# A retention layer and two expert layers in one kernel: carry and inner product summed in PSUM, a table made on chip, low bits on ScalarE, PSUM divided, late loads held back

## The chip, the cores and the metric

The kernel runs on one core of one Trainium2 chip. The metric is the device time of one execution in microseconds; of the kernel before, three runs took 606.27, 607.22 and 610.22 us, the median being 607.22.

## The reference, cut to what matters

```python
# q, k, v: [2, 8, 768, 64] float32
gamma = 1.0 - 2.0 ** (-5.0 - np.arange(H))
for t in range(S):                       # retention, state per (batch, head): 64 x 64
    state = gamma[None, :, None, None] * state + einsum('bhd,bhe->bhde', k[:, :, t], v[:, :, t])
    y[:, :, t] = scale * einsum('bhd,bhde->bhe', q[:, :, t], state)
x = y as [1536 tokens, 512]
h = x @ w_in;  x = (max(h, 0) + log1p(exp(-abs(h)))) @ w_out         # layer 0, d_ff = 2048
h = x @ w_in2; x = (h * clip(h + 3, 0, 6) / 6) @ w_out2              # layer 1, d_ff = 2048
```

The four weight matrices arrive as float64. Every product is computed to nearly float32 exactness, from operands that are split into a high half of reduced precision (fp32r) and a low half, the rest.

## The kernel before, in words

**Retention.** The sequence is cut into chunks of 128 tokens, six per batch, so there are 12 units, counted from 0 (`attend`, line 368). A unit loads k, q and v (256 KB each, `load`, line 392). TensorE turns k and q by transposes (called T below, `turned`, line 408); ScalarE copies k out of PSUM (kT) and VectorE multiplies q by the table `tq_sb` (qT). VectorE scales v (vs). TensorE forms scores in two halves (S, `scores`, line 426), and VectorE masks them (pt). TensorE forms the state's increments (D, `product`, line 440), and VectorE adds them to the running states (st, lines 449 to 466). Then come the carry product from the states (C, `carry`, line 468, into a bank `oc`) and the inner product of pt and vs (I, `inner`, line 478, into two banks `oi`). ScalarE copies `oc` to a buffer of the pool e, VectorE adds the banks `oi` to it into a buffer of the pool g (lines 496 to 508), ScalarE rounds this to the high half `x_hi`, and VectorE subtracts for the low half `x_lo` (lines 509 to 511).

**Expert layers.** Tokens are taken in three blocks of 512, d_ff in 16 slices of 128. `gemm1` (line 517) is a block of 12 products of 512 columns into one bank h, `gemm2` (line 555) a block of 12 into four accumulator banks. Between them ScalarE and VectorE apply the activation and split it into `hi` and `lo`. There are 96 blocks of each of the two.

**Weights.** 64 weight slices (`weight`, line 229) are fetched as words of 64 bits (512 KB) into one of three buffers `raw`. ScalarE scales the high word and VectorE clamps it; the low word's bits are added either by ScalarE (`bits`, a Relu activation, line 257) followed by `sign` and `shift` on VectorE, or by VectorE alone (`shifted`, `sign`, `merge`). `BITS` (line 148) chooses: VectorE alone for every fourth slice. The result `cv` is split into the halves `w`: for the slices that `BY_DVE` (line 145) names VectorE subtracts (`low`), for the others ScalarE writes the negative and an accumulating DMA from POOL's queue adds (`add`).

**The order.** A planner (`Plan`, line 24) is given every task with its engine, cost, due time and the buffers and banks that it takes and gives back. `run` (line 70) issues, on the engine that can start first, the task with the earliest due time among those that can start about as soon. So the kernel's text does not show the order; all engine calls go through `keep_in_program_order` (line 41), which is why every row of the profile bears L41. The banks of PSUM are one pool of eight, which `places` (line 61) hands out: to a task of two banks two neighbours, else the banks that are free first. SP's queue carries all loads in order, POOL's the accumulating DMAs.

The lines that set due times of the units in TensorE's order are these:

```python
for i, block in enumerate(([("Tk", u), ("Tq", u)], [("D", u)], [("S", u)], [("C", u), ("I", u)])):
    gaps.setdefault(start + int((4 * n + i) * per), []).extend(block)
```

Of the kernel before, what the change touches and what calls it, by code (L numbers as in the profile page):

```python
# [22 lines left out]
class Plan:  # L23
# [5 lines left out]
    class Task:  # L29
        def __init__(self, n, eng, cost, fn, after, due, take, give, load):  # L30
# [13 lines left out]
    def __init__(self, tc):  # L44
        self.tc, self.tasks, self.pools, self.users, self.slot = tc, [], {}, {}, {}
        self.tensor, self.vector, self.scalar, self.gpsimd, self.sync = (
            self.Engine(self, getattr(tc.nc, e)) for e in ("tensor", "vector", "scalar", "gpsimd", "sync"))
# [6 lines left out]
    def add(self, eng, cost, fn, after=(), due=0.0, take=(), give=(), load=0.0):  # L54
        t = self.Task(len(self.tasks), eng, cost, fn, after, due, take, give, load)
        self.tasks.append(t)
        for k in t.give:
            self.users.setdefault(k, []).append(t)
        return t

    def places(self, pool, keys, at=None):

        times = [(x if at is None else max(x, at), i) for i, x in enumerate(self.pools[pool]) if x is not None]
        if len(keys) == 2:
            have = {i: x for x, i in times}
            two = min(((max(x, have[i + 1]), -i) for i, x in have.items() if i + 1 in have), default=None)
            return two and [-two[1], 1 - two[1]]
        return [i for _, i in sorted(times)[:len(keys)]] if len(times) >= len(keys) else None

    def run(self, log=None):  # L70
        free = {"PE": 0.0, "DVE": 0.0, "ACT": 0.0, "POOL": 0.0, "SP": 1.2}
        line = 0.0
        todo = {e: sorted((t for t in self.tasks if t.eng == e), key=lambda t: (t.due, t.n)) for e in free}
        left = {k: len(v) for k, v in self.users.items()}
        for _ in self.tasks:
            best = None
            for e, ts in todo.items():
                found = []
                for t in ts[:80]:
                    if any(a.done is None for a in t.after):  # L80
                        continue
                    at = max([free[e]] + [a.done + (self.LAG[a.eng] if a.eng != e else 0.0) for a in t.after])
# [22 lines left out]
            if t.load:  # L105
                line = max(line, end + 1.2) + t.load
                end = line + 0.5
# [17 lines left out]
def kernel(ctx, tc, q, k, v, w1_in, w1_out, w2_in, w2_out, tq, tk, tcc, out):  # L125
# [17 lines left out]
    AHEAD = 3  # L143

    def BY_DVE(n):
        return n < 6 or n < 2 * NF and n % 3 == 1

    def BITS(n):
        return n % 4 != 1
# [26 lines left out]
    nc.pool("bank", 8)  # L176
    conv = [[("conv", m, i) for i in range(9)] for m in range(2)]
# [21 lines left out]
    for u in range(START):  # L199
        pe += [("S", u), ("D", u)] + ([("Tk", u + 1), ("Tq", u + 1)] if u + 1 < START else []) + [("C", u), ("I", u)]  # L200
# [7 lines left out]
    spread(range(START, FIRST), 0, 1.0)  # L208
# [126 lines left out]
    small = fixed.tile([P, HALF + H + NP], F32, name="small")  # L335
    mask, tk_sb, tc_sb = small[:, :HALF], small[:, HALF:HALF + H], small[:, HALF + H:]
# [14 lines left out]
    def table(dst, src, when):  # L351
        return nc.add("SP", 0.45, lambda: nc.sync.dma_start(out=dst, in_=src), [], when, load=1.3 if dst is tq_sb else 0.1)

    def both(keys):
        a, b = sorted(nc.slot[x][1] for x in keys)
        return banks[:, a:b + 1:b - a, :NP * HALF].rearrange("p x (n t) -> p x n t", n=NP)

    def sub(keys, j):
        i = sorted(nc.slot[x][1] for x in keys)[j]
        return banks[:, i, :NP * HALF].rearrange("p (n t) -> p n t", n=NP)  # L360
# [4 lines left out]
    part = [slice(j * HALF, (j + 1) * HALF) for j in range(2)]  # L365
    tables, ready = {}, {}

    def attend(u):
# [6 lines left out]
        def task(eng, cost, fn, after, when, take=(), give=(), load=0.0):  # L375
            return nc.add(eng, cost, fn, after, when, [(p, k) for p, k in take], list(give) + mine, load)
# [15 lines left out]
        def load(n, when, parts=1):  # L392
            return task("SP", 0.45 * parts, fetch(n, parts), [], when, take=own(n), load=1.32)
# [9 lines left out]
        if u == 0:  # L403
            tables["q"] = table(tq_sb, tq, begin + 2)
            tables["k"] = table(tk_sb, tk, begin + 2.1)
            tables["c"] = table(tc_sb, tcc, begin + 3.1)

        def turned(n):
# [5 lines left out]
        tp = task("PE", cost["Tk"], turned("k"), [ik], d["Tk"], take=[("bank", ("kP", u))])  # L414
# [3 lines left out]
        qt = task("DVE", PSX, lambda: nc.vector.tensor_tensor(tile_of("qT"), bank(("qP", u)), tq_sb, ALU.mult), [tp, tables["q"]],  # L418
# [3 lines left out]
            [iv, tables["k"]], d["D"] - 1.2, take=own("vs"), give=[("v", u)])  # L422

        sc, ds, oi = ([(n, j, u) for j in range(2)] for n in ("sc", "ds", "oi"))

        def scores():
# [7 lines left out]
            tile_of("pt").rearrange("p n (g t) -> p g n t", g=2).rearrange("p g n t -> p g n t"), both(sc),  # L434
            mask.rearrange("p (a n t) -> p a n t", a=1, n=1).to_broadcast([P, 2, NP, HALF]), ALU.mult), [s],
            d["I"] - 1.2, take=own("pt"), give=sc)
# [20 lines left out]
        if not last:  # L457
# [8 lines left out]
            ready["end", u] = task("DVE", 0.42, faded, [e, tables["c"]], due["C", u + 1] - 2.0, give=[end[1]])  # L466
# [8 lines left out]
        c = task("PE", cost["C"] / (1 + first), carry, [qt, sm, None if first else ready["end", u - 1]], d["C"],  # L475
                 take=[("bank", ("oc", u))], give=[mid[1], ("qT", u)] + ([] if first else [("end", u - 1)]))

        def inner():
            for h in range(H):
                g, p = h % 2, h // 2  # L480
                for j in range(2):
                    nc.tensor.matmul(sub(oi, j)[part[g], p, :], tile_of("vs")[part[j], h, :], tile_of("pt").rearrange(
                        "p n (g t) -> p g n t", g=2)[part[j], g, p, :])

        n = task("PE", cost["I"], inner, [pt, vs], d["I"], take=[("bank", x) for x in oi], give=[("pt", u), ("vs", u)])
# [4 lines left out]
        def split(t):  # L490
            return t.rearrange("p n (j t) -> p j n t", j=2)

        def of(n):
            return at_slot((n, u)).rearrange("p (n t) -> p n t", n=NP)

        if first:
            o0 = task("ACT", 0.35, lambda: nc.scalar.activation(split(of("on"))[:, 0], sub(oi, 0), AF.Copy), [n], d["I"] + 0.7,
                      take=[("g", ("on", u))], give=oi)
            o1 = task("ACT", 0.35, lambda: nc.scalar.activation(split(of("oe"))[:, 1], split(bank(("oc", u)))[:, 1], AF.Copy), [c],
                      d["I"], take=[("e", ("oe", u))], give=[("oc", u)])  # L500
# [155 lines left out]
```

## Time and profile before

| | us |
|---|---|
| median of three runs | 607.22 |
| the profiled execution, its own time | 606.65 |
| its span, first to last instruction | 604.5 |
| TensorE busy | 582.9 |
| VectorE busy | 335.9 |
| ScalarE busy | 304.7 |
| POOL busy | 44.3 |

The span is what the views of the trace cover; 2.15 us of the execution lie around it. Instructions of one engine overlap a little, so starts, not ends, tell how fast a queue moves. PE is TensorE, DVE VectorE, ACT ScalarE, SP the queue of loads and stores. A time in brackets is idle time of the engine before an instruction, with the instruction that ended it.

### The profile page before, as it was taken

Reading aid. Unit: us, or ns where it says so; the run is one execution under the profiler, and the core shown is the slowest. Engines: PE = TensorE matmul, PEld = TensorE weight load, DVE = VectorE, ACT = ScalarE, POOL = GpSimd, SP = SyncE. Lnnn points to the kernel's source line nnn. Section 1 sums busy time; section 2 is a strip of 40 time slices with the busy share of each in tenths; the row PEclk is TensorE's granted clock in tenths of the full one; section 3 lists DMA queues with packets and bytes.
Section 4 is the critical chain, followed back from the end, with each engine's and each line's share of the span. In section 5 each row is a group of like instructions: output and inputs, shape, how many; then the busy total and the mean of one; then the engine's idle time right before and its main releaser. Section 6 shows DMA issues by size and latency. Waiting matters only on the chain.

```text
span 604.5 us, 9654 instructions
## 1 busy us (share of the span) xinstructions
PE 582.9 (96%) x3891; PEld 478.2 (79%) x3891; DVE 335.9 (56%) x584; ACT 304.7 (50%) x516; POOL 44.3 (7%) x57
## 2 busy tenths in 40 slices
PE   7698889999999999999999999999999999999997
PEld 6576668878788888888888887888888888888886
DVE  4899898995655333376677985622422222322223
ACT  2468877994533333476779996622222222222220
POOL 0001111120000000011122221100000000000000
PEclk9899989999999999999999999999999999999999
DMA  8997776966210100046588987510100000100001
GB/s 193 237 252 199 195 183 158 241 180 137 54 37 21 51 0 1 1 105 157 152 196 212 247 211 176 130 18 0 71 1 1 0 1 0 71 0 1 0 1 69
DMA packets 68364, 59.87 MB, mean 99 GB/s; under 512 B 39776, under 2 KB 56416, under 8 KB 68320
## 3 DMA queue, kind: packets, MB, share of 16 engines
q1 hardware_dynamic: 61264, 46.41, 26.9%
q0 software_dynamic: 7056, 12.85, 12.4%
q8 instruction: 30, 0.49, 0.4%
q14 instruction: 14, 0.11, 0.1%
HBM read 43.26 MB, written 3.15 MB: 77 GB/s over the span
## 4 chain that ended last, share of the span: by engine, by line
PE 76%; DVE 10%; DMA 6%; ACT 5%; issue 3%; SPq 1%; DVEq 0%; ACTq 0%
PE banks L41 76%; DVE cv L41 5%; DMA raw<-in_moe_w_out_dram 3%; DMA raw<-in_moe_w_in_dram 2%; DVE raw L41 1%; ACT w L41 1%; DVE g L41 1%; DVE lo L41 1%; ACT raw L41 1%; DMA v<-in_v_dram 1%; ACT cv L41 1%; ACT e L41 1%; SPq L41 1%; DVE x_lo L41 1%; DVE w L41 1%
## 5 line engine op out<-in xcount | busy, mean ns | idle before, releaser
L41 PE MATMUL banks<-x_hi,w 128*128 128x512 f32 x768 | 254.8, 393 | 5.0 <-ACT kT L41 2.2
L41 PEld LDWEIGHTS banks<-x_hi,w 128*128 128x128 f32 x768 | 144.8, 189 | 37.1 <-DVE g L41 2.5
L41 PE MATMUL banks<-x_lo,w 128*128 128x512 f32 x384 | 150.2, 391 | 0.0
L41 PE MATMUL banks<-hi,w 128*128 128x512 f32 x384 | 127.5, 393 | 0.8 <-ACT w L41 0.5
L41 PE MATMUL banks<-w,hi 128*128 128x512 f32 (+1 forms) x386 | 118.3, 388 | 0.0
L41 DVE SCALAR_TENSOR_TENSOR g<-e,banks 128x512 f32<-128x512 f32 x48 | 33.0, 688 | 114.1 <-ACT e L41 114.0
L41 ACT ACTIVATE e<-banks,three 128x512 f32<-128x512 f32 x48 | 32.9, 686 | 124.6 <-PE banks L41 116.7
L41 DVE SCALAR_TENSOR_TENSOR cv<-raw,cv 128x512 uint32<-128x512 uint32 x128 | 87.5, 689 | 6.7 <-ACT cv L41 4.2
L41 DVE TENSOR_TENSOR lo<-g,hi 128x512 fp32r<-128x512 f32 x96 | 66.2, 690 | 44.7 <-ACT hi L41 43.4
L41 ACT ACTIVATE hi<-g 128x512 fp32r<-128x512 f32 x96 | 60.5, 630 | 49.8 <-DVE g L41 33.3
L41 PEld LDWEIGHTS banks<-hi,w 128*128 128x128 f32 x384 | 72.0, 188 | 17.0 <-ACT w L41 0.9
L41 PEld LDWEIGHTS banks<-x_lo,w 128*128 128x128 f32 x384 | 72.6, 189 | 14.7
L41 PEld LDWEIGHTS banks<-w,hi 128*128 128x128 f32 x386 | 72.4, 188 | 14.9
L41 ACT ACTIVATE w<-cv 128x512 fp32r<-128x512 f32 x113 | 68.3, 624 | 16.7 <-DVE cv L41 16.2
L41 PE MATMUL banks<-lo,w 128*128 128x512 f32 x192 | 75.1, 391 | 1.4 <-DVE lo L41 1.4
L41 PE MATMUL banks<-w,lo 128*128 128x512 f32 (+1 forms) x193 | 74.9, 388 | 0.0
L41 POOL DMA_DIRECT2D w<-cv x49 | 43.3, 887 | 348.9 <-ACT w L41 208.3
L41 ACT ACTIVATE g<-banks 128x512 f32<-128x512 f32 (+1 forms) x50 | 29.2, 584 | 54.7 <-PE banks L41 54.2
L41 ACT ACTIVATE raw<-raw 128x512 f32<-128x512 f32 x64 | 42.7, 667 | 8.7 <-DMA raw<-in_moe_w_out_dram 5.1
L41 PEld LDWEIGHTS banks<-lo,w 128*128 128x128 f32 x192 | 36.0, 188 | 9.5 <-DVE lo L41 2.2
L41 DVE SCALAR_TENSOR_TENSOR g<-g,e 128x512 f32<-128x512 f32 x48 | 33.1, 690 | 16.3 <-ACT e L41 15.7
L41 PEld LDWEIGHTS banks<-w,lo 128*128 128x128 f32 x193 | 36.3, 188 | 7.5
(58 smaller groups left out, 340.2 us busy)
## 6 DMA issues: line engine op xcount, KB each, us to landing
raw<-in_moe_w_in_dram SPq DMA_DIRECT2D x32, 512.0 KB, 4.1
raw<-in_moe_w_out_dram SPq DMA_DIRECT2D x32, 512.0 KB, 4.3
w<-cv POOLq DMA_DIRECT2D x49, 256.0 KB, 4.4
out_dram<-e SPq DMA_DIRECT2D x11, 256.0 KB, 2.0
q<-in_q_dram SPq DMA_DIRECT2D x8, 256.0 KB, 5.0
v<-in_v_dram SPq DMA_DIRECT2D x8, 256.0 KB, 4.9
k<-in_k_dram SPq DMA_DIRECT2D x7, 256.0 KB, 4.7
raw<-in_k_dram SPq DMA_DIRECT2D x4, 256.0 KB, 3.2
```

Of the source, the lines that this page charges most:

```text
L41: return self.plan.tc.keep_in_program_order(getattr(self.engine, op)(*args, **kwargs))
```

## The change: what it does

- `inner` writes its two banks with `start` at the first p of each half; `carry` then adds into the same banks with `start=False`, after a tiny VectorE copy of those banks into `seen`. C now stands behind I. The ScalarE copy and the VectorE add go; `x_hi` and `x_lo` are made straight from PSUM.
- The table of q is no longer loaded (256 KB); one small load brings three tables of [128, 20] in all, VectorE spreads the gammas over 512 columns, TensorE turns them, ScalarE copies them to `tq_sb`.
- `BITS` is always true, so ScalarE makes the low bits of the 16 slices that VectorE had. `BY_DVE` names 19 slices instead of 15, all in layer 0.
- PSUM: h takes bank 0 or 1, the accumulators banks 4 to 7; units take the pair 2 and 3, and the first four units any pair. From unit 5 on, T waits for the C of the unit before.
- Loads of units 4 to 11 may not be planned earlier than 8 us after the time at which they were due. The planner counts loads of SP and POOL as sharing the transfer engines.

```diff
-        return n < 6 or n < 2 * NF and n % 3 == 1
+        return n < 6 or n < 2 * NF and n % 2 == 1
     def BITS(n):
-        return n % 4 != 1
+        return True
...
+        if kind == "h":
+            return [[0], [1]]
+        if kind == "acc":
+            return [[4, 5, 6, 7]]
+        pairs = [[2, 3]] + ([[4, 5], [6, 7], [0, 1]] if u < START else [])
+        return pairs if len(keys) == 2 else [[i] for x in pairs for i in x]
...
-            for i, block in enumerate(([("Tk", u), ("Tq", u)], [("D", u)], [("S", u)], [("C", u), ("I", u)])):
-                gaps.setdefault(start + int((4 * n + i) * per), []).extend(block)
+            for i, block in enumerate(("T", "S", "D", "I", "C")):
+                gaps.setdefault(start + int((5 * n + i) * per), []).extend([("Tk", u), ("Tq", u)] if block == "T" else [(block, u)])
...
-            return task("SP", 0.45 * parts, fetch(n, parts), [], when, take=own(n), load=1.32)
+            return task("SP", 0.45 * parts, fetch(n, parts), [], when, take=own(n), load=1.32, hold=HOLD + when if u >= START else 0.0)
...
+        def inner():
+            for p in range(NP):
+                for g in range(2):
+                    for j in range(2):
+                        nc.tensor.matmul(sub(o, j)[part[g], p, :], tile_of("vs")[part[j], 2 * p + g, :], split(tile_of("pt"))[part[j], g, p, :],
+                                         start=(p == 0), stop=(p == NP - 1))
+        def between():
+            nc.vector.tensor_copy(seen.rearrange("p (x n t) -> p x n t", x=2, n=1), both(o)[:, :, :1, :1])
...
-                        nc.tensor.matmul(bank(("oc", u))[part[g], p, part[j]], w[part[g], p, :], tile_of("qT")[part[g], p, part[j]])
+                        nc.tensor.matmul(sub(o, j)[part[g], p, :], w[part[g], p, :], tile_of("qT")[part[g], p, part[j]],
+                                         start=False, stop=True, skip_group_check=True)
...
-            on = task("DVE", PSX, lambda: nc.vector.tensor_tensor(split(of("on")), split(of("oe")), both(oi), ALU.add),
-                      [n, o1], d["I"] + 1.0, take=[("g", ("on", u))], give=oi + [("oe", u)])
...
+        o2 = task("ACT", PSX, lambda: nc.scalar.activation(split(hi), both(o), AF.Copy), [c], need - 1.5, give=o)
+        o3 = task("DVE", PSX, lambda: nc.vector.tensor_tensor(split(lo), both(o), split(hi).bitcast(F32), ALU.subtract), [o2],
+                  need - 0.8, give=o)
```

What stands in VectorE's queue around the second weight slice (buffers raw_1 and cv_1) and the third unit's result; before:

```order
L41 TENSOR_SCALAR raw_1_73<-raw_1_73 128x512
L41 TENSOR_SCALAR cv_1_76<-raw_1_73 128x512
L41 TENSOR_TENSOR w_79<-cv_0_75,w_79 128x512
L41 SCALAR_TENSOR_TENSOR cv_1_76<-raw_1_73,cv_1_76 128x512
L41 TENSOR_TENSOR vs_0_132<-v_0_126,small 128x512
L41 SCALAR_TENSOR_TENSOR cv_1_76<-raw_1_73,cv_1_76 128x512
L41 TENSOR_TENSOR g_106<-e_103,banks 128x2x4x64
```

and in the kernel as changed:

```order
L42 COPY seen<-banks 128x2
L42 TENSOR_SCALAR raw_1_73<-raw_1_73 128x512
L42 TENSOR_TENSOR st_137<-st_137,small 128x256
L42 TENSOR_TENSOR w_79<-cv_0_75,w_79 128x512
L42 SCALAR_TENSOR_TENSOR cv_1_76<-raw_1_73,cv_1_76 128x512 x2
L42 TENSOR_TENSOR qT_0_130<-banks,tq_sb 128x512
L42 TENSOR_TENSOR vs_0_132<-v_0_126,small 128x512
```

The shift `cv_1<-raw_1` and the add `g<-e,banks` are gone, `seen` has come, and the fourth unit's qT and vs stand behind the second slice. Counted from the first clamp (`raw_0<-raw_0`) to the twelfth `lo<-g,hi`, VectorE's list held 185 instructions and holds 178. By kind, before and now: word operations `cv<-raw,cv` 57 and 56, `cv<-raw` 8 and 0, `raw<-raw` 29 and 29, `e<-g` 13 and 13, `g<-g,e` 12 and 12, `lo` 12 and 12, `x_lo` 7 and 7, `g<-e,banks` 5 (and one of half size) and 0, qT 4 and 5, vs 5 and 5, pt 5 and 5, `w<-cv,w` 13 and 14, state operations of 256 columns 14 and 14, `seen` 0 and 6. To the sixteenth `lo`, `cv<-raw,cv` has 64 and 64, `w<-cv,w` 15 and 19, and the state operations 14 and 15.

SP's queue around the first weights (raw_0 to raw_2 are the three buffers of fetched slices; k_0, q_0, v_0 at this place are the fourth unit's); before:

```order
L41 DMA q_0_120<-in_q_dram 128x8x64
L41 DMA raw_0_72<-in_moe_w_in_dram 128x4x256
L41 DMA raw_1_73<-in_moe_w_in_dram 128x4x256
L41 DMA raw_2_74<-in_moe_w_in_dram 128x4x256
L41 DMA v_0_126<-in_v_dram 128x8x64
L41 DMA k_0_123<-in_k_dram 128x8x64
L41 DMA q_1_121<-in_q_dram 128x8x64
L41 DMA v_1_127<-in_v_dram 128x8x64
L41 DMA k_1_124<-in_k_dram 128x8x64
L41 DMA q_2_122<-in_q_dram 128x8x64
L41 DMA v_2_128<-in_v_dram 128x8x64
L41 DMA k_2_125<-in_k_dram 128x8x64
```

and now:

```order
L42 DMA raw_2_74<-in_moe_w_in_dram 128x4x256
L42 DMA q_0_120<-in_q_dram 128x8x64
L42 DMA v_0_126<-in_v_dram 128x8x64
L42 DMA k_0_123<-in_k_dram 128x8x64
L42 DMA k_1_124<-in_k_dram 128x8x64
L42 DMA q_1_121<-in_q_dram 128x8x64
L42 DMA v_1_127<-in_v_dram 128x8x64
L42 DMA raw_0_72<-in_moe_w_out_dram 128x1024
L42 DMA raw_1_73<-in_moe_w_in_dram 128x4x256
L42 DMA raw_2_74<-in_moe_w_in_dram 128x4x256
L42 DMA k_0_123<-in_k_dram 128x8x64
L42 DMA q_0_120<-in_q_dram 128x8x64
```

Before, eight loads of units followed the fourth unit's q and the first three slices here, and one more before the next slice; now six loads follow the first three slices, and the next three slices come ahead of unit 5's k.

On TensorE, from unit 5 on, a block of products stands between I and C and another behind C. At the C of unit 5 (`qT,st`) and the turn of unit 6's k and q (`ident`) the list reads now:

```order
L42 MATMUL banks<-qT_0_130,st_136 64x64 x8
L42 MATMUL banks<-x_hi_66,w_88 128x512
L42 MATMUL banks<-x_lo_69,w_88 128x512
L42 MATMUL banks<-x_hi_66,w_88 128x512 x2
L42 MATMUL banks<-x_lo_69,w_88 128x512
L42 MATMUL banks<-x_hi_66,w_88 128x512 x2
L42 MATMUL banks<-x_lo_69,w_88 128x512
L42 MATMUL banks<-x_hi_66,w_88 128x512 x2
L42 MATMUL banks<-x_lo_69,w_88 128x512
L42 MATMUL banks<-x_hi_66,w_88 128x512
L42 MATMUL banks<-ident,k_1_124 128x128 x4
L42 MATMUL banks<-ident,q_1_121 128x128 x4
```

and of unit 4 and the block before it, in the kernel before:

```order
L41 MATMUL banks<-x_hi_66,w_81 128x512
L41 MATMUL banks<-qT_0_130,st_138 64x64 x8
L41 MATMUL banks<-qT_0_130,st_136 64x64 x8
L41 MATMUL banks<-pt_0_134,vs_0_132 64x64 x16
L41 MATMUL banks<-ident,k_2_125 128x128 x4
L41 MATMUL banks<-vs_1_133,k_2_125 64x64 x8
L41 MATMUL banks<-ident,k_0_123 128x128 x4
```

There C, I and the next units' turns of k stood side by side; now a whole block of products lies between C and the next turn, behind units 4 two blocks.

## Rows read from the trace of the kernel before

**Rows 1.** Page, busy us, share of the span and instructions of each engine.
```profile
PE 582.9 (96%) x3891; PEld 478.2 (79%) x3891; DVE 335.9 (56%) x584; ACT 304.7 (50%) x516; POOL 44.3 (7%) x57
```

**Rows 2.** Stretches: us; busy PE, PEld, DVE, ACT, POOL; granted clock; DMA share; GB/s.
```profile
20.86:128.50 107.64, 95.01 (x949) 75.44 (x946) 99.62 (x186) 84.19 (x149) 13.58 (x15) 0.95 0.81 204
33.90:128.50 94.60, 86.46 (x777) 68.09 (x769) 87.03 (x163) 76.82 (x136) 13.58 (x15) 0.98 0.78 203
128.50:340.00 211.50, 211.45 (x1386) 174.14 (x1387) 126.77 (x222) 122.29 (x210) 17.47 (x20) 1.00 0.39 93
250.00:372.00 122.00, 121.67 (x537) 100.42 (x537) 89.81 (x157) 97.72 (x171) 23.61 (x27) 1.00 0.71 174
```

**Rows 3.** Waits of PE from 20 to 130: total us, times, longest.
```profile
PE banks L41 <- ACT g L41: 2.3, 2, 1.2
PE banks L41 <- DVE lo L41: 1.4, 1, 1.4
```

**Rows 4.** Time line of PE: start us, us, instruction, idle before.
```profile
25.05 1.09 PE L41 MATMUL banks<-ident,k 128*128 128x128 f32 x4 [4.03 <-DVE cv L41]
...
82.24 0.69 PE L41 MATMUL banks<-pt,vs 64*64 64x64 f32 x32
...
125.80 0.61 PE L41 MATMUL banks<-hi,w 128*128 128x512 f32 x2
...
126.48 0.61 PE L41 MATMUL banks<-hi,w 128*128 128x512 f32 x2
128.54 0.50 PE L41 MATMUL banks<-lo,w 128*128 128x512 f32 x1 [1.45 <-DVE lo L41]
...
366.15 0.50 PE L41 MATMUL banks<-x_hi,w 128*128 128x512 f32 x1 [0.33 <-DVE g L41]
```

**Rows 5.** Time line of DVE at two places.
```profile
70.45 0.68 DVE L41 TENSOR_TENSOR qT<-banks,tq_sb 128x512 f32<-128x512 f32 x1
71.05 0.42 DVE L41 TENSOR_SCALAR e<-g 128x512 uint32<-128x512 uint32 x1
71.38 0.68 DVE L41 TENSOR_TENSOR x_lo<-g,x_hi 128x512 fp32r<-128x512 f32 x1
...
91.28 0.68 DVE L41 TENSOR_TENSOR x_lo<-g,x_hi 128x512 fp32r<-128x512 f32 x1
```

**Rows 6.** Groups by form, whole span: count, busy us, mean ns, idle before.
```profile
L41 ACT ACTIVATE cv<-raw,half 128x512 uint32<-128x512 uint32 x48 | 36.5, 760 | 2.4 <-DMA w<-cv 2.4
L41 DVE TENSOR_TENSOR x_lo<-banks,x_hi 128x512 fp32r<-128x512 f32 x12 | 7.9, 687 | 1.1 <-ACT x_hi L41 1.1
L41 DVE TENSOR_TENSOR g<-e,banks 128x512 f32<-128x512 f32 x10 | 6.8, 685 | 0.8 <-ACT e L41 0.6
L41 DVE TENSOR_SCALAR cv<-raw 128x512 uint32<-128x512 uint32 x16 | 6.8, 426 | 0.4
L41 ACT ACTIVATE e<-banks 128x512 f32<-128x512 f32 x10 | 5.9, 594 | 6.3 <-PE banks L41 6.3
L41 DVE TENSOR_TENSOR pt<-banks,small 128x512 f32<-128x512 f32 x8 | 5.5, 687 | 1.8 <-PE banks L41 1.7
L41 DVE COPY small<-e 64x64 f32<-64x64 f32 x2 | 0.4, 188 | 0.8 <-POOL e masks.py:66 0.8
```

**Rows 7.** DMA: GB/s in 40 slices, and the issue of the table.
```profile
GB/s 193 237 252 199 195 183 158 241 180 137 54 37 21 51 0 1 1 105 157 152 196 212 247 211 176 130 18 0 71 1 1 0 1 0 71 0 1 0 1 69
...
tq_sb<-in_tq_dram SPq DMA_DIRECT2D x1, 256.0 KB, 4.2
```

**Rows 8.** Time line of ACT near 366 us: start us, us, instruction, idle before.
```profile
363.65 1.15 ACT L41 ACTIVATE w<-cv 128x512 fp32r<-128x512 f32 x2 [1.51 <-DVE cv L41]
364.71 0.67 ACT L41 ACTIVATE e<-banks,three 128x512 f32<-128x512 f32 x1
365.83 0.78 ACT L41 ACTIVATE cv<-raw,half 128x512 uint32<-128x512 uint32 x1
366.49 0.64 ACT L41 ACTIVATE hi<-g 128x512 fp32r<-128x512 f32 x1
```

More of the change, by code (lines that the diff above doesn't have):

```diff
@@ L61, in places @@
     def places(self, pool, keys, at=None):
[L63 to L68, printed above, removed]
+        times = {i: x if at is None else max(x, at) for i, x in enumerate(self.pools[pool]) if x is not None}
+        if pool in self.groups:
+            ok = [g for g in self.groups[pool](keys) if all(i in times for i in g)]
+            return min(ok, key=lambda g: max(times[i] for i in g), default=None)
+        return sorted(times, key=lambda i: (times[i], i))[:len(keys)] if len(times) >= len(keys) else None
     def run(self, log=None):
         free = {"PE": 0.0, "DVE": 0.0, "ACT": 0.0, "POOL": 0.0, "SP": 1.2}
-        line = 0.0
+        line = {"SP": 0.0, "POOL": 0.0}
         todo = {e: sorted((t for t in self.tasks if t.eng == e), key=lambda t: (t.due, t.n)) for e in free}
@@ L124, with kernel @@
 @with_exitstack
-def kernel(ctx, tc, q, k, v, w1_in, w1_out, w2_in, w2_out, tq, tk, tcc, out):
+def kernel(ctx, tc, q, k, v, w1_in, w1_out, w2_in, w2_out, table, out):
     nc = Plan(tc)
@@ L373, in attend, with task @@
         mine = second if ph else arena
-        def task(eng, cost, fn, after, when, take=(), give=(), load=0.0):
-            return nc.add(eng, cost, fn, after, when, [(p, k) for p, k in take], list(give) + mine, load)
+        def task(eng, cost, fn, after, when, take=(), give=(), load=0.0, hold=0.0):
+            return nc.add(eng, cost, fn, after, when, [(p, k) for p, k in take], list(give) + mine, load, hold)
         def tile_of(n):
@@ L403, in attend @@
         if u == 0:
-            tables["q"] = table(tq_sb, tq, begin + 2)
-            tables["k"] = table(tk_sb, tk, begin + 2.1)
-            tables["c"] = table(tc_sb, tcc, begin + 3.1)
+            ready["t"] = nc.add("SP", 0.45, lambda: nc.sync.dma_start(out=tables, in_=table), [], begin - 1, load=0.1)
+            t = nc.add("DVE", 0.62, spread_out, [ready["t"]], begin, take=[("e", "wide")])
+            t = nc.add("PE", 0.46, wide_turned, [t], 0.0, take=[("bank", ("tqP", 0))], give=["wide"])
+            ready["q"] = nc.add("ACT", ACP, lambda: nc.scalar.activation(tq_sb, bank(("tqP", 0)), AF.Copy), [t], begin, give=[("tqP", 0)])
         def turned(n):
@@ L472, in carry @@
                     for g in range(2):
-                        nc.tensor.matmul(bank(("oc", u))[part[g], p, part[j]], w[part[g], p, :], tile_of("qT")[part[g], p, part[j]])
[L475 to L485, printed above, removed]
+                        nc.tensor.matmul(sub(o, j)[part[g], p, :], w[part[g], p, :], tile_of("qT")[part[g], p, part[j]],
+                                         start=False, stop=True, skip_group_check=True)
+        n = task("PE", cost["I"], inner, [pt, vs], d["I"], take=[("bank", x) for x in o], give=[("pt", u), ("vs", u)])
+        n = task("DVE", 0.1, between, [n], d["I"] + 0.5)
+        c = task("PE", cost["C"] / (1 + first), carry, [qt, n, sm, None if first else ready["end", u - 1]], d["C"],
+                 give=[mid[1], ("qT", u)] + ([] if first else [("end", u - 1)]))
         ch, off = divmod(u * C, CH)
```

93 lines of the change are left out of this document (46 added, 47 removed).

## The prediction

> **What bounds the kernel now.** I read the views from coarse to fine: the engine lines of the page, then busy time by stretch, then who TensorE waits for, then the time line at those waits, then single instructions. The engine lines [rows 1] show TensorE busy for 582.9 of 604.5 us, so at most 21.6 us can be won by feeding it better; the change leaves its matmuls as many as they were. The stretches [rows 2] say where those microseconds lie. From 128.5 to 340 us TensorE is busy 211.45 of 211.50 us, and from 250 to 372 us 121.67 of 122: nothing to win there. Between 20.86 us (VectorE's first clamp of a weight) and 128.5 us it is busy 95.01 of 107.64, while VectorE is busy 99.62 of the same 107.64 us, ScalarE 84.19 and the DMA engines 0.81 of their time. From the first product of the expert layers (33.9 us) on, TensorE idles 94.60 - 86.46 = 8.1 us. VectorE is the fullest engine of that stretch, and TensorE's waits there [rows 3] are for results that go through ScalarE's or VectorE's queue: ACT g, DVE lo. On the time line [rows 4] the last of them ends at 128.54 us, where the low half `lo` of an activation comes late; behind that TensorE runs without a gap. So what counts is how soon VectorE gets through the instructions that stand between its first clamp and that `lo`, the twelfth.
>
> **The change part by part.**
>
> *VectorE's queue, the main term.* Instructions are issued closer than they last: a 512-column form of 0.68 us gives way to the next after 0.60 us, a light one of 0.42 us (tensor-scalar) after 0.33 us [rows 5]; I take 0.60 and, with the lag before some light ones, 0.36, and 0.40 for the 256-column forms. The order lists before show 185 instructions from the first clamp to the twelfth `lo`: 120 of the 512-column kind, 50 light, 15 of 256 columns: 72 + 18 + 6 = 96 us of issue, which took 107.6 us; each us of issue is worth 107.6/96 = 1.12 us of time. In the new order 178 stand there. Gone are 8 shifts of the high word (0.43 us each [rows 6], because ScalarE now takes all low bits), 5 full adds of carry and inner product (0.69 us) and one half add; one word operation more falls behind the place. Come are one qT, one low half of a weight (4 more in the whole first matrix pair, 1 of them ahead of this place) and 6 tiny copies `seen`. In issue: -8 x 0.36 - 5 x 0.60 - 0.36 - 0.60 + 2 x 0.60 + 6 x 0.10 = -5.0 us, times 1.12 = **-5.7 us**. If instead the sixteenth `lo` (all first-layer weights made) decides, three more low halves and a state operation count: -2.2 us, times 1.12 = -2.5 us.
>
> *`seen`.* No row shows a copy of two columns out of PSUM. The copy of 64 columns (0.188 us [rows 6]) is the nearest, so it lies between 0 and that; I take 0.10, the middle, as it has two columns. The wait itself is dearer: behind `seen` in VectorE's queue stand the next unit's vs and weight words, which all wait until TensorE has done the inner product, and the carry product waits for `seen`. The nearest row is pt, which waits for TensorE in the same way: 1.8 us of idle time in 8 [rows 6], so 0 to 6 x 0.2 = 1.4 us. I take 0, because a block of products stands between inner product and carry from unit 4 on.
>
> *The low and high half read PSUM.* From PSUM the low half takes 687 ns [rows 6], from SBUF 0.68 us [rows 5]. That is nothing on VectorE, and the ScalarE copy `e<-banks` (594 ns) goes, 8 times before 128.5 us.
>
> *Table and loads.* The 256 KB table tq is loaded no more [rows 7]. In its slice the DMA engines moved 237 GB/s [rows 7], so all behind it comes 0.262 MB/237 GB/s = 1.1 us sooner: **-1.1 us**, as unit 3's k (the fourth unit), for which TensorE stood 4.03 us [rows 4], and the first weights arrive through the same queue. What takes its place (a broadcast copy on VectorE, four transposes, a ScalarE copy) runs beside TensorE's 16 idle transposes, before the first k. Loads of units 4 to 11 now stand behind the weights on SP. Unit 5's loads still stand on SP ahead of a weight whose products TensorE runs before it turns unit 5's k, and that weight must be converted besides, so I cost the delay at nothing; without that cover a late load costs what the late k cost, up to 4.0 us. Four accumulating DMAs fewer on POOL's queue: nothing, as low halves by VectorE take their place.
>
> *Low bits on ScalarE.* Eight more in each layer, 0.76 us each [rows 6], the next starting 0.66 us later [rows 8]: +5.3 us per layer. In the first layer eight copies and four negatives go, so ScalarE's load (84.19 of 107.64) stays. In the second nothing leaves ScalarE: 97.72 of 122 us becomes 103. There one TensorE wait shows [rows 4]: at 366.15 us it stood 0.33 us for DVE g, which stood behind ACT e, which had waited behind two weight conversions for VectorE [rows 8]. As the shift that those waited for is one instruction shorter now, I put the price between 0 and 5.3 us and take **+1.0**, near the 0.33 that the row shows.
>
> *PSUM divided.* Product banks 0 and 1, accumulators 4 to 7, one pair (2, 3) for units from 4 on. The next unit's k cannot be turned until the low half of this one has read the pair. Taken at 0: in the new VectorE order 10 to 14 instructions lie from `seen` to that low half, about 5 us, and TensorE has two blocks of products there, each 12 products some 0.227 us apart [rows 4], 2.7 us. The price without cover is the rival below.
>
> Sum: -5.7 - 1.1 + 1.0 = -5.8. The profiled execution took 606.65 us (2.15 outside its span), the median of three runs 607.22; I go from the former: **600.9 us**, its own range 598 to 604.
>
> **The rivals.**
>
> *TensorE fed without gaps.* Later weights come earlier in VectorE's new order, and two products of the second token block stand before the last of the first. If all idle time from 33.9 to 128.5 us goes: -8.1 - 1.1 = -9.2, near 597.4; and if the granted clock, 0.98 of its 2.4 GHz in that stretch [rows 2], stays full as well, 0.02 x 94.6 = 1.9 us more: 595.5. For it: at 128.5 us TensorE needs only 5 us of lead. Against: VectorE's queue still holds 91 us of issue up to the twelfth `lo`.
>
> *ScalarE becomes the bound.* The rows say: low bits cost VectorE a shift of 426 ns and cost ScalarE an activation of 760 ns [rows 6]. If ScalarE ends last from 250 to 372 us, its extra 5.3 us come in full behind the 6.8 won: 606.65 - 6.8 + 5.3 = 605.2, no change. For it: the waits of [rows 8]; against: 24 us of its 122 are idle. The Trainium skill speaks for this rival ("ScalarE: Activation LUTs", Rules for kernel authors): relu and the like belong on VectorE, not on ScalarE, and these low bits are made by a Relu activation. By that rule the move loses on balance and this rival's time stands; by the rows it frees the fuller engine, and the forecast stands.
>
> *Slower: the pair of banks.* Before, unit 5's inner product ended at 82.93 us and its low half at 91.96 [rows 4, 5], 9.0 us later, without hurting anyone, as other banks were free. Without add and copy (1.3 us) 7.7 are left. In the new order one block of 2.7 us stands between the carry of units 5 and 6 and the next turn of k, two behind unit 4. If the queues are as long as they were, TensorE stands 2 x 5.0 + 2.3 = 12.3 us: 606.65 - 6.8 + 12.3 = 612.2. It decides once the low half comes more than one block after the carry. Against it: the new order puts it sooner in the queue.
>
> **How the numbers follow.** The forecast has 0.50, gap-free feeding 0.15, ScalarE 0.21, the pair 0.14. A measurement here tells about 1% (6.1 us, so 601.15 and 613.3) from no change. The forecast lies so near to that edge that 0.28 of its 0.50 fall on the faster side; with 0.15 that makes faster 0.43. Same: 0.22 + 0.21 = 0.43. Slower: 0.14, of which the part beyond 613.3 needs the pair and ScalarE together, or a late load besides. The range goes from gap-free feeding (595) up into the third rival, with a part of its 12.3 us: 609.
>
> **What would show it.** Right: TensorE's idle time from 33.9 us to its last wait falls from 8.1 to under 4; the twelfth `lo` ends near 122 us; VectorE has no `g<-e,banks` adds of units and no `cv<-raw` shifts; the k of unit 3 is used near 24 us. Wrong: TensorE waiting for x_lo or kT before a turn of k (the pair); waits for DVE g or ACT e over 1 us between 320 and 372 us (ScalarE); a first product later than 36 us that is not made good; a DMA among TensorE's releasers (held loads).

## The result, and the profile after

| | before | changed |
|---|---|---|
| median of six executions, us | 607.96 | 603.24 |
| profiled execution, its own time | 606.65 | 602.95 |
| its span | 604.5 | 601.2 |
| first product of the expert layers starts | 33.91 | 36.61 |
| last product ends | 600.67 | 597.20 |

The ratio is 0.9918, interval 0.9889 to 0.9948: 0.8% faster. The forecast was 5.8 us from the profiled execution; that execution gained 3.7, the medians 4.7.

The engine line of the page and the four stretches of [rows 2] read now (us; busy PE, PEld, DVE, ACT, POOL; granted clock; DMA share; GB/s):

```profile
PE 586.3 (98%) x3895; PEld 479.1 (80%) x3895; DVE 326.4 (54%) x573; ACT 305.5 (51%) x515; POOL 40.3 (7%) x53
...
20.86:128.50 107.64, 102.95 (x1043) 82.40 (x1044) 100.04 (x191) 88.11 (x154) 10.57 (x12) 0.95 0.77 198
33.90:128.50 94.60, 93.30 (x863) 74.36 (x860) 88.38 (x168) 81.95 (x143) 10.57 (x12) 1.00 0.78 202
128.50:340.00 211.50, 210.84 (x1375) 171.29 (x1373) 121.58 (x215) 121.52 (x209) 17.39 (x20) 1.00 0.40 97
250.00:372.00 122.00, 120.49 (x530) 98.93 (x529) 89.03 (x153) 103.84 (x182) 24.29 (x28) 1.00 0.74 180
```

TensorE idles 94.60 - 93.30 = 1.3 us from 33.9 to 128.5 us, where it idled 8.1. Its busy time rose from 582.9 to 586.3 us with four instructions more; 3.0 of these 3.4 us lie ahead of the first product (27.66 us busy there, 24.66 before), where the mean granted clock was 0.81, before 0.90. Its waits from 20 to 130 us, in answer to [rows 3] (total us, times, longest):

```profile
PE banks L42 <- DVE pt L42: 2.1, 2, 1.3
PE banks L42 <- DVE st L42: 1.2, 1, 1.2
PE banks L42 <- DVE qT L42: 0.8, 1, 0.8
PE banks L42 <- DVE seen L42: 0.7, 1, 0.7
PE banks L42 <- ACT g L42: 0.5, 1, 0.5
```

All but the last lie before the first product. Inside the products, up to 128.54 us, 7.9 us of waits (for g, kT, w and lo) have become this one of 0.47 us for ACT g. On TensorE's time line the places of [rows 4] and of the start are these (start us, us, instruction, idle before):

```profile
4.92 1.06 PE L42 MATMUL banks<-ident,e 128*128 128x128 f32 x4
6.67 0.66 PE L42 MATMUL banks<-ident,k 128*128 128x128 f32 x4 [0.69 <-ACT tq_sb L42]
...
24.10 1.11 PE L42 MATMUL banks<-ident,q 128*128 128x128 f32 x4
26.05 1.12 PE L42 MATMUL banks<-ident,k 128*128 128x128 f32 x4 [0.84 <-DVE qT L42]
...
30.38 1.13 PE L42 MATMUL banks<-pt,vs 64*64 64x64 f32 x32 [1.29 <-DVE pt L42]
31.44 1.11 PE L42 MATMUL banks<-ident,k 128*128 128x128 f32 x4
...
33.34 1.29 PE L42 MATMUL banks<-qT,st 64*64 64x64 f32 x30
...
35.98 0.69 PE L42 MATMUL banks<-vs,k 64*64 64x64 f32 x32 [0.83 <-DVE pt L42]
36.61 0.50 PE L42 MATMUL banks<-x_hi,w 128*128 128x512 f32 x1
...
77.90 0.50 PE L42 MATMUL banks<-x_hi,w 128*128 128x512 f32 x1
...
80.84 0.69 PE L42 MATMUL banks<-vs,k 64*64 64x64 f32 x32
...
121.33 0.50 PE L42 MATMUL banks<-x_hi,w 128*128 128x512 f32 x1 [0.47 <-ACT g L42]
...
126.69 0.61 PE L42 MATMUL banks<-hi,w 128*128 128x512 f32 x2
...
129.41 0.39 PE L42 MATMUL banks<-hi,w 128*128 128x512 f32 x1
...
339.91 0.50 PE L42 MATMUL banks<-x_hi,w 128*128 128x512 f32 x1 [0.66 <-DVE g L42]
...
362.94 0.50 PE L42 MATMUL banks<-x_hi,w 128*128 128x512 f32 x1 [0.85 <-DVE g L42]
```

VectorE's twelfth `lo`, which ended about 128.5 us, stands at 119.74 and ends at 120.43:

```profile
119.74 0.69 DVE L42 TENSOR_TENSOR lo<-g,hi 128x512 fp32r<-128x512 f32 x1
```

From this time line one can draw up where the 600.67 - 597.20 = 3.47 us at the last product come from. I walked both lists of matmuls from the first product to the last and split the time into idle time (the bracketed values), units' pieces and products:

| us | before | changed | difference |
|---|---|---|---|
| first product starts | 33.91 | 36.61 | +2.70 |
| idle after it | 8.26 | 1.98 | -6.28 |
| units' pieces between products | 27.39 | 27.39 | 0 |
| one block at the low clock (86.16) | 1.58 | 0 | -1.58 |
| all products otherwise | 529.53 | 531.22 | +1.69 |
| last product ends | 600.67 | 597.20 | -3.47 |

The block at 86.16 us of the kernel before took 4.53 us to the next start, against 2.95 of others like it:

```profile
86.16 0.69 PE L41 MATMUL banks<-x_hi,w 128*128 128x512 f32 x1 [2.20 <-ACT kT L41]
...
90.69 0.69 PE L41 MATMUL banks<-vs,k 64*64 64x64 f32 x32
```

After the 2.20 us of waiting for kT the granted clock was 0.79 from 84 to 92 us, so part of it ran at 1.2 GHz. The last difference comes from breaks: a row of products is interrupted by a unit's piece 37 times, before 22 times. To the next start, the last product ahead of a piece and the first behind one take 0.08 and 0.11 us more than the 0.227 of the others, 2.3 us more in all than before; fewer restarts behind waits take 0.6 off. A block followed by a block takes 2.72 us from first start to first start (126.69 to 129.41), one followed by a piece 2.94 (77.90 to 80.84).

### The profile page after: what moved, and what is told of

Its sections match the earlier page's. It is cut to its first block, busy times and chain, and to the rows that moved or that the text cites. A ratio compares the mean times of both kernels' runs of the same rounds, so it can differ in the third digit from the quotient of the medians.

```text
span 601.2 us, 9628 instructions
## 1 busy us (share of the span) xinstructions
PE 586.3 (98%) x3895; PEld 479.1 (80%) x3895; DVE 326.4 (54%) x573; ACT 305.5 (51%) x515; POOL 40.3 (7%) x53
## 4 chain that ended last, share of the span: by engine, by line
PE 85%; DVE 4%; DMA 4%; ACT 4%; issue 1%; POOL 0%; DVEq 0%; SPq 0%; ACTq 0%; POOLq 0%
PE banks L42 85%; DMA raw<-in_moe_w_out_dram 4%; DVE cv L42 2%; ACT raw L42 1%; ACT w L42 1%; ACT cv L42 1%; ACT g L42 0%; ACT hi L42 0%; ACT e L42 0%; DVE raw L42 0%; DMA out_dram<-e 0%; DVE qT L42 0%; DVE g L42 0%; DVE pt L42 0%; DVE st L42 0%
## 5 line engine op out<-in xcount | busy, mean ns | idle before, releaser
L42 ACT ACTIVATE w<-cv 128x512 fp32r<-128x512 f32 x109 | 65.5, 624 | 8.0 <-DVE cv L42 7.6
L42 POOL DMA_DIRECT2D w<-cv x45 | 39.2, 872 | 349.4 <-ACT w L42 203.6
L42 ACT ACTIVATE g<-banks 128x512 f32<-128x512 f32 x48 | 28.6, 595 | 53.6 <-PE banks L42 51.1
L42 ACT ACTIVATE cv<-raw,half 128x512 uint32<-128x512 uint32 x64 | 48.2, 758 | 0.0
```

The source lines that it names most:

```text
L42: return self.plan.tc.keep_in_program_order(getattr(self.engine, op)(*args, **kwargs))
```

## The experiments

All times are compared with the kernel before by ratio; its median was between 606.99 and 607.96 us beside these runs. First product, idle time after it (a wait just ahead of it is not counted), breaks and the end of the twelfth `lo` are from the time lines of the profiled executions.

| | median us | ratio, interval | first product | idle after | breaks | twelfth lo |
|---|---|---|---|---|---|---|
| changed kernel | 603.24 | 0.9918 (0.9889 to 0.9948) | 36.61 | 2.0 | 37 | 120.4 |
| e1 low bits back | 605.23 | 0.9963 (0.9940 to 0.9985) | 36.64 | 2.1 | 39 | 123.0 |
| e2 before, weights alone | 603.39 | 0.9947 (0.9922 to 0.9972) | 36.59 | 4.4 | 24 | 124.9 |
| e3 before, carry alone | 608.87 | 1.0035 (1.0014 to 1.0057) | 35.17 | 8.4 | 30 | 127.5 |
| e4 few pieces | 600.52 | 0.9902 (0.9873 to 0.9931) | 34.59 | 3.2 | 23 | 117.2 |
| e5 first units' carry apart | 604.37 | 0.9957 (0.9932 to 0.9983) | 38.53 | 2.6 | 38 | 126.2 |
| e6 any bank | 603.50 | 0.9923 (0.9896 to 0.9949) | 36.24 | 2.5 | 32 | 120.2 |
| e7 loads not held | 604.10 | 0.9933 (0.9908 to 0.9958) | 38.51 | 1.5 | 38 | 121.7 |
| e8 256 KB more loaded | 603.74 | 0.9933 (0.9909 to 0.9958) | 37.59 | 1.5 | 37 | 121.4 |
| e9 unit 4 later | 602.99 | 0.9915 (0.9885 to 0.9946) | 31.88 | 1.1 | 40 | 118.6 |
| e10 e4, unit 4 behind a carry | 603.53 | 0.9932 (0.9907 to 0.9958) | 36.73 | 3.9 | 24 | 119.8 |
| e11 low halves back | 605.89 | 0.9968 (0.9940 to 0.9997) | 37.10 | 4.7 | 35 | 125.8 |
| e12 e4 and e9 together | 608.13 | 1.0001 (0.9978 to 1.0023) | 37.63 | 2.8 | 25 | 121.8 |

**e1, the low bits undone.**

```diff
     def BITS(n):
-        return True
+        return n % 4 != 1
```

> The changed kernel with one part undone: VectorE makes the low bits of every fourth slice again. VectorE then has 186 instructions from its first clamp to the twelfth lo (changed kernel 178, before 185). Theory A, VectorE's queue length sets TensorE's waits: idle time after the first product goes from 2.0 us back to 6 to 8, and the time rises by 3 to 5 us, to 606 to 608. Theory B, the gain came from the new order of units and banks, not from the shorter queue: idle time stays under 3 us, the two waits near 340 and 363 us (0.66 and 0.85 us) go with ScalarE's extra load, and the time is 601 to 603.5, as the changed kernel's 603.24 or 1.5 us less.

It fell between the two. The twelfth `lo` ended 2.6 us later, near the 8 x 0.36 x 1.12 = 3.2 us that the prediction gives to the eight shifts, and the ratio rose by 0.0045 (some 2.7 us; the intervals overlap a little); counted from VectorE's first clamp, as the prediction counts, the way to that `lo` took 103.80 us against 99.82. But TensorE's waits did not come back. So the edit is worth about what the forecast took, and not by the way that it gave: in the profiled execution the last product came 1.8 us later, of which waits are 0.1, products 1.1 and units' pieces 0.5. A count of VectorE's instructions (186 here, 185 before) does not tell how long TensorE waits. Theory B's other half fell too: with ScalarE back at 97.94 us of the 122, TensorE still waits at 358.98 us, 1.25 us for DVE g. ScalarE's time line there:

```profile
355.93 0.67 ACT L42 ACTIVATE raw<-raw 128x512 f32<-128x512 f32 x1 [1.91 <-DMA raw<-in_moe_w_in_dram]
356.50 1.14 ACT L42 ACTIVATE w<-cv 128x512 fp32r<-128x512 f32 x2
357.54 0.66 ACT L42 ACTIVATE e<-banks,three 128x512 f32<-128x512 f32 x1
```

The activation `e`, from which VectorE makes g, stands behind weight work that waited 1.91 us for a fetch.

**e2, the weights' part alone**, on the kernel before: `BITS` always true and `n % 2` for `n % 3` in `BY_DVE`.

> The kernel before with two edits alone: ScalarE makes all low bits, and VectorE's low halves are chosen as in the changed kernel. VectorE has 176 instructions to the twelfth lo (before 185). Theory A (queue length): idle time after the first product falls from 8.3 us to under 3.5, the first product stays at 33.9 us, the blocks stay as undivided as before, and the time is 601 to 604 against 608 of before. Theory B (order of units and banks): idle time stays over 6 us and the time is within 2 us of before. Both: waits for DVE g or ACT e of 1 to 2 us in all between 320 and 372 us, if it is ScalarE's load that makes them.

Theory A's time came (603.39), with 4.4 us of idle time, above its 3.5. This part alone is some two thirds of the gain by the ratio, though the intervals overlap. The waits for DVE g between 320 and 372 us, put at 1 to 2 us if ScalarE's load makes them, came to 0.21 with ScalarE busy for 103.24 of the 122 us: its load alone does not make them. The run also shows that a late first product (36.59, where 33.9 was expected) needs neither the carry nor the table: with unit 3's k turned at 24.39 us, TensorE stood 3.85 us before that unit's increments.

**e3, the carry's part alone**, on the kernel before: the diff's `inner`, `between`, `carry`, `o2`, `o3` and the five pieces, with banks as before.

> The kernel before with the carry's part alone: carry added in PSUM behind the inner product and a copy seen, units in five pieces, banks undivided. VectorE has 183 instructions to the twelfth lo (before 185). Theory A: idle time after the first product stays over 6 us. Theory C, on the start: with the carry behind inner product and seen nothing of TensorE covers the making of pt in the first units, so the first product comes 1.5 to 3 us later than 33.9, and the time is 608 to 611, no gain. Rival to C, that the banks or the held loads made the first product late: it stays within 0.7 us of 33.9 and the time is 605 to 608.

Slower, as A and C said together, but mostly from another place than C named: the first product came 1.26 us later (C: 1.5 to 3), and then TensorE met one long wait. TensorE's time line:

```profile
51.57 0.94 PE L41 MATMUL banks<-vs,k 64*64 64x64 f32 x32
58.10 1.13 PE L41 MATMUL banks<-pt,vs 64*64 64x64 f32 x32 [5.60 <-DVE pt L41]
```

Unit 5's inner product stands in TensorE's order before the next block, and VectorE makes its pt after eleven instructions of weights, which fill 50.76 to 57.36 us; the last of them and pt:

```profile
56.03 1.42 DVE L41 SCALAR_TENSOR_TENSOR cv<-raw,cv 128x512 uint32<-128x512 uint32 x2
57.36 0.68 DVE L41 TENSOR_TENSOR pt<-banks,small 128x512 f32<-128x512 f32 x1
```

The five adds fewer are worth nothing if the order puts a unit's step into TensorE's queue before VectorE gets to it. Here the twelfth `lo` gained 1.0 us (1.7 counted from the first clamp).

**e4, fewer breaks.** The pieces of a unit from 4 on are T, S with D, I, C, three apart instead of five, so that C falls beside the next T; any bank may be used.

```diff
...
-            for i, block in enumerate(("T", "S", "D", "I", "C")):
-                gaps.setdefault(start + int((5 * n + i) * per), []).extend([("Tk", u), ("Tq", u)] if block == "T" else [(block, u)])
+            for i, block in enumerate(([("Tk", u), ("Tq", u)], [("S", u), ("D", u)], [("I", u)], [("C", u)])):
+                gaps.setdefault(start + int((3 * n + i) * per), []).extend(block)
...
```

> The changed kernel with any bank for any purpose and the units from 4 on issued in fewer pieces: 23 breaks in the row of expert products instead of 37 (before 22). Theory D, each break costs TensorE 0.11 to 0.22 us (a block of 12 followed by a unit's piece takes 2.95 us to the next start, one followed by a block 2.72): 14 breaks fewer give 1.5 to 3.1 us, so 600.1 to 601.7. Rival: a break costs nothing beyond the piece itself, or the waits for masks and copies that the pieces hid come back: 603 or more, with idle time after the first product over 3 us in the second case.

The time fell into theory D's range, 600.52 us, but not by breaks alone. The products took 529.0 us in all instead of 531.2, which is 0.16 us for each of 14 breaks fewer; the units' pieces, standing together, took 0.9 us more. On balance that is 1.3 us or 0.09 a break, beside 0.11 for the 15 that the change added (1.69 us). The waits rose by 1.2 us, which uses that up. The last product came 2.05 us earlier, as much as the first (34.59 against 36.61), so the gain of the profiled execution is that of the start; e10 below, with the same pieces and a first product at 36.73, is no faster than the changed kernel. It is the fastest kernel of the study, though its interval overlaps that of the changed kernel.

**e5, the first units' carry apart.** For units 0 to 3 the lines of the kernel before (bank `oc`, ScalarE copy, VectorE add) stand again, C ahead of I.

> The changed kernel with the first four units' carry put back into a bank of its own ahead of the inner product, with the ScalarE copy and the VectorE add; units from 4 on stay as changed. Theory C, in the first units no product covers pt and seen, so the carry behind them delays the first product: the first product comes at 34 to 35 us instead of 36.6, waits for pt and seen before it fall from 2.9 us to under 1.2, idle after it stays under 3 us (179 VectorE instructions to the twelfth lo, against 178), and the time is 601 to 602.5 where the changed kernel took 603.24. Rival, that banks or VectorE's weight words make the start late whatever the carry does: the first product at 36 us or later and 603 to 605.

Theory C did not come, and the rival's numbers did: the first product came at 38.53 us, later than ever. Unit 3's k was turned at 27.11 us (26.05), and TensorE ran at the low clock level from 28 to 40 us. The profiled execution took 609.44 us, 5 above the median, so its start may not be typical; the median by itself lies outside C's range.

**e6, banks undivided.** `bank_groups` gives any neighbouring pair, any single bank, any four.

> The changed kernel with PSUM undivided: any pair for units, any bank for the products, any four for the accumulators; 32 breaks among the products instead of 37. Theory D (a break costs 0.14 us, from 14 fewer breaks and 1.9 us less product time in e4): product time 0.7 us less. The bank theory of the prediction, dividing PSUM costs or gains nothing by waits of TensorE for x_lo or kT: time 602 to 603.2. Rival, the division itself feeds TensorE better by keeping two banks for the products: idle time after the first product goes over 4 us, and the time is 604 or more.

603.50 us, within what can be told of the changed kernel; the products took 0.9 us less for five breaks fewer, the pieces 0.6 more and the waits 0.5 more. That the division feeds or starves TensorE is not to be seen.

**e7, loads not held**, `hold=0.0`.

> The changed kernel without holding late loads back: unit loads stand ahead of weights on SP again. The prediction's term, that holding costs nothing: first product within 0.7 us of 36.6 and time 602.5 to 604. Rival, held loads bring the weights sooner and so feed TensorE: without it, idle after the first product over 3.5 us with waits for w, and 604.5 to 607.

The time is 0.1 above the first range (604.10), the first product far outside it (38.51), and idle time stayed at 1.5 with one wait for w, of 0.36 us: the held loads do not feed TensorE by bringing the weights sooner. But the last product came 2.0 us later (599.21), as much as the first; whether holding gains that at the start, or this order does, is not shown.

**e8, 256 KB more.** The list of every engine's work is the same; one load more stands behind the first q.

> The changed kernel with 256 KB more loaded behind the first unit's q, into a buffer that nothing reads, in the place where the table stood before; every engine's order of work is the same. The prediction's term, all behind it comes 1.1 us later on the path: the first product and the end 0.8 to 1.3 us later, 604.0 to 604.6. Rival, the start is set by TensorE's own chain and VectorE, with the loads ahead of it: first product within 0.4 us and time within 0.6 of the changed kernel's 603.24.

First product and last product came 0.98 and 1.01 us later (598.21 for the latter), and unit 3's k landed at 23.7 us instead of 22.8: in the traces the prediction's term holds. The median rose by 0.5 alone, which is within the rival's 0.6.

**e9, unit 4 later**, `spread(range(START, FIRST), 2, 0.8)` for `0, 0.8`.

> The changed kernel with the fourth row of units (4 to 7) due two blocks of products later: unit 4's scores, increments and the rest now stand behind the first two products, and VectorE's qT of unit 4 behind unit 3's x_lo. Theory E, the first product came late because unit 4's turn, qT and scores stood in the in-order queues ahead of unit 3's carry and x_lo (1.6 us of waiting for the carry behind that turn, 1.1 us for qT): the first product comes at 33.5 to 35 us instead of 36.6, and the time is 601 to 602.3 (three breaks more cost 0.4). Rival F, unit 3's k and TensorE's clock at the low level set the start: the first product at 36 us or later, 602.8 to 604.5.

The first product came at 31.88 us, earlier than theory E had it, and the profiled span was 598.6 us, yet the median is 602.99, in rival F's range. The executions differ in the granted clock: five with a mean of 0.997 have spans of 597.5 to 599.3 us, six with 0.986 to 0.993 have 601.2 to 604.5.

**e10, unit 4 behind unit 3's carry**: e4, with that carry among the conditions of unit 4's turns.

> As e4 (any bank, few pieces, 600.52 us), and unit 4's k and q may not be turned before unit 3's carry; 24 breaks. Theory E: the first product at or before 34.6 us, as in e4 or up to 1.5 us earlier, 599 to 600.5. Rival F: unit 3's k or the clock decides, first product 35 to 37.5 us and 600.5 to 602.5.

Against theory E the first product came at 36.73 us: with the turn moved, the inner product still waited 1.36 us for pt, and the carry took 1.98 us (1.15 at the high clock, in e9). The median, 603.53, is above the ranges of both theories.

**e11, low halves back**, `n % 3` for `n % 2` in `BY_DVE`.

> The changed kernel with its low halves of weights chosen as before: 15 by VectorE instead of 19, the others by POOL's accumulating DMAs. VectorE has 179 instructions to the twelfth lo and 202 to the sixteenth (changed kernel 178 and 206). Theory A (queue length): within 0.8 us of 603.24 or faster. Rival: a low half by accumulating DMA lands later, and TensorE waits for w; idle after the first product 3.5 us or more, and 604 to 607.

The rival's numbers came, not its wait: 605.89 us and 4.7 us of idle time, but none of it for w. VectorE's list to the twelfth `lo` is one instruction longer, and yet that `lo` ended 5.4 us later. Of that, 1.0 us lies ahead of the first clamp, and 3.4 us are VectorE standing idle from there to the `lo` (7.3 against 4.0): from 20 to 130 us it waited 3.0 us for ScalarE's scaled word and 2.3 for its `cv` (changed kernel: 0.2 and 0.5). ScalarE in turn waited 3.1 us for fetched slices (0.2) and 1.0 us for an accumulating DMA to give back `cv` (1.8 us in the kernel before, none in the changed one). From 33.9 to 128.5 us the DMA engines were busy for 0.84 of the time, against 0.78; that the added DMAs made the fetches late fits this, but no run isolates it.

**e12, both.** e4, with `spread(range(START, FIRST), 3, 1.3)`, and unit 4's turns behind unit 3's x_lo.

> As e4 (any bank, few pieces), with the units from 4 on due three blocks later and unit 4's k and q turned only after unit 3's x_lo; 25 breaks. Theories D and E together: the first product at 31.5 to 33.5 us as in e9, product time near 529 us as in e4, idle time after the first product under 3.5 us, and 598 to 600.5, under both the changed kernel and e4's 600.52. Rival G, the time goes by TensorE's clock in the first 40 us, which no order of the units holds at the high level: an execution with 10 us or more at the low level comes out at 601.5 or more, whatever the pieces.

No gain at all, 608.13 us, with idle time after the first product at 2.8 us as hoped. VectorE's time line shows what came ahead of the x_lo for which the first product waited 1.83 us:

```profile
33.70 1.42 DVE L43 SCALAR_TENSOR_TENSOR cv<-raw,cv 128x512 uint32<-128x512 uint32 x2
35.03 0.42 DVE L43 TENSOR_SCALAR raw<-raw 128x512 f32<-128x512 f32 x1
35.56 1.42 DVE L43 SCALAR_TENSOR_TENSOR cv<-raw,cv 128x512 uint32<-128x512 uint32 x2
36.90 0.68 DVE L43 TENSOR_TENSOR x_lo<-banks,x_hi 128x512 fp32r<-128x512 f32 x1
```

With unit 4 out of the way the planner filled VectorE with weight words instead. TensorE's clock was low for 17 us of the first 44 here, for 3.4 in e9 (stretches of 4 us, the missing share of the clock times two). Rival G holds for this run.

## Why the prediction was right, step by step

The time was in the range and on the forecast's side; 603.24 us is 2.3 above 600.9. That it is so near is in part luck: in the profiled execution waits and clock gave 3.4 us more than the main term, and the start, the breaks and the second layer's waits cost 5.7 us more than the sum had for them. By terms:

- **VectorE's queue, -5.7.** The sign "the twelfth `lo` ends near 122 us" came (120.4; from the first clamp 99.82 us instead of 107.64, 7.8 less; the prediction's 5.0 x 1.12 is 5.6), and the idle time fell under 4, to 1.3. The gain at this term was larger than forecast: 8.26 - 0.33 - 0.47 = 7.5 us of waits up to 128.5 us, and 1.6 us of low clock, which is what the rival "TensorE fed without gaps" had taken (8.1 and 1.9). The cause was only half right. The weights' part feeds TensorE by itself (e2: idle time from 8.3 to 4.4 us). The shifts' share holds at the `lo` (e1: 2.6 us measured, 4.0 from the first clamp, 3.2 forecast), but without them TensorE waited no longer. The adds' share does not hold: alone they gave 1.0 us at the `lo` and a slower kernel (e3). Nor does the length of the list set the `lo`: lists of 176 to 179 instructions ended between 117.2 and 126.2 us. And the sentence "Four accumulating DMAs fewer on POOL's queue: nothing" failed: choosing four low halves for VectorE is worth 2.65 us of median (e11 against the changed kernel; the intervals just overlap). The parts do not add up: undone singly, low bits and low halves cost 0.45% and 0.50%, both alone on the kernel before give 0.53% (e2), the carry alone costs 0.35% (e3), and all together give 0.82%.
- **Table and loads, -1.1.** The size is right (e8: 1.0 us; unit 3's k landed at 22.8 us, before at 24.9), though the 237 GB/s are those of the second slice: the table was issued at 2.32 us, in the first, with 193. The path was wrong. The table's four transposes and a wait for `tq_sb` stand ahead of the first k (6.67 us above), which the prediction had covered by idle transposes; before it was turned 2.0 us earlier:

```profile
4.66 0.60 PE L41 MATMUL banks<-ident,k 128*128 128x128 f32 x4
```

And "the k of unit 3 is used near 24 us" was wrong: it was used at 26.05. q and k of that unit are turned into the same bank in the new order, so k waited 0.84 us for VectorE to read q (the bank is read from that wait; the rows do not number the banks). Then S, pt and I followed without cover, unit 4's turn (31.44) stood ahead of the carry (33.34), and the first product came at 36.61, 2.7 us later than before and 3.8 later than forecast. The sign "a first product later than 36 us that is not made good" came in its first half; the shorter waits made it good by 80 us.
- **What the sum left out.** The units' pieces went from four to five, which the prediction described and did not price: 15 breaks more, +1.69 us (0.11 us a break; e4 gives 0.09 on balance). With the start (+2.7) and the waits of the second layer (+1.2) this is why 7.5 + 1.6 us of gain became 3.5.
- **Low bits on ScalarE, +1.0.** Two waits of 0.66 and 0.85 us for DVE g took the place of one of 0.33: +1.2. Added up they make the sign "over 1 us" come. ScalarE's load came as forecast, 103.84 us of 122. But e1 has a wait of 1.25 us there without the extra load and e2 one of 0.21 with it, so the price is not that of the low bits; in e1 it is an activation behind weight work that waits. The rival "ScalarE becomes the bound" (605.2) did not come. The rule of the Trainium skill ("ScalarE: Activation LUTs", Rules for kernel authors), relu on VectorE, would have the move lose; here e1, which moves a quarter of the low bits back, is slower by 0.45%, with intervals that overlap a little: the measurement leans to ScalarE where VectorE is the fuller engine.
- **PSUM divided, 0.** Behind unit 0 no wait for x_lo or kT appears among TensorE's releasers, and e6 is level with the changed kernel. The rival of the bank pair (612.2) is out. (The inner product that it took from 82.24 us is unit 6's, not unit 5's.)
- **`seen`, 0.** A copy took 157 ns where 100 were taken; TensorE waited for it once, 0.73 us, before the first product. VectorE waited 4.1 us for TensorE in the twelve copies:

```profile
L42 DVE COPY seen<-banks 128x2 f32<-128x2 f32 x12 | 1.9, 157 | 4.2 <-PE banks L42 4.1
L42 ACT ACTIVATE cv<-raw,half 128x512 uint32<-128x512 uint32 x64 | 48.2, 758 | 0.0
```

- **Holding loads, 0.** No DMA stands among TensorE's releasers, and e7 has no more idle time; its later start is open.

What stays open is the start. The changed kernel and the twelve runs put the first product between 31.88 and 38.53 us, each in one profiled execution. Neither the table (e2), the carry (e5) nor unit 4's turn (e10, e12) explains it alone. Nor does the clock: up to 44 us TensorE stood at the low level for 13.7 us in the changed kernel, 6.8 before and 3.4 in e9, but also for 3.4 in e11, whose first product came at 37.10.

## What to carry to other kernels

When an edit makes a planner lay out the work anew, price the layout too: count how often a row of products is broken (about 0.1 us each on balance here) and follow the chain to the first product step by step. A shorter queue on the fullest engine pays only if the order keeps each consumer behind its producer; the carry's part alone, with its five adds fewer, made this kernel slower, the weights alone gave two thirds of the gain. Small edits of the same plan moved the time by up to 7.6 us (e12 against e4), so a gain of 1% should be tried with one part undone at a time before a part is credited with it.

## What the runs showed that was not expected

- A break in a row of 512-column products costs TensorE time beyond the piece itself: 2.94 us against 2.72 for the block ahead of it, 0.09 to 0.11 us on balance.
- The mean granted clock differs from one execution of a kernel to the next (e9: 0.986 to 0.997). Up to the last product, the profiles show the low level in the first 44 us, and in the kernel before, e2 and e3 also behind later waits. Over all timed executions of this study, 0.001 less of mean clock goes with 0.34 us more of span (215 executions, correlation -0.58, each kernel against its own mean). In the changed kernel the clock was at 0.50, the level of 1.2 GHz, from 24 to 32 us; ahead of that TensorE was busy for 0.76 of the 2 us from 20 to 22:

```profile
20.00:22.00 2.00, 0.76 (x43) 0.56 (x32) 1.97 (x6) 2.00 (x4) 0.00 (x0) 1.00 0.74 163
...
24.00:28.00 4.00, 3.16 (x44) 2.33 (x44) 3.93 (x8) 2.28 (x4) 0.00 (x0) 0.50 0.92 255
28.00:32.00 4.00, 2.71 (x79) 2.40 (x72) 3.84 (x9) 0.00 (x0) 0.00 (x0) 0.50 0.29 100
```
